# A fused two-layer transformer on one NeuronCore: a new hand-written order of 3,078 steps, other engines, PSUM banks and cross-engine turns, 76 waits of TensorE placed elsewhere, 17 waits added

## The chip, the cores and the metric

The kernel runs on one core of a Trainium2 chip. The metric is the device time of one execution in microseconds (us). The core has a matrix engine (PE in the profile, TensorE in words), whose weight loads are shown apart (PEld), a vector engine (DVE), an engine for activation functions (ACT), a general engine (POOL) and a queue that issues transfers (SP). Each engine runs its own list of instructions in order. They keep step by semaphores: an instruction can wait until a counter has reached a value.

## The reference, cut to what matters

```python
x = A_x                                           # [1, 2048, 512], bf16
for layer in range(2):                            # the same weights in both
    q, k, v = split(layernorm(x) @ wqkv)          # 32 heads of 16
    p = softmax(where(0 <= i - j < 256, q @ k.T / 4, -1e9))
    x = x + (p @ v) @ wo
    h = gelu(layernorm(x) @ w1 + b1)              # 512 -> 1792, tanh form
    x = x + h @ w2 + b2                           # 1792 -> 512
```

## The kernel before, in words

The 2,048 rows of x are 16 tiles of 128 rows. Both layers are laid end to end, so there are 32 tiles (tau 0 to 31). Attention works on pairs of tiles, 16 blocks b; its queries look back at most 256 positions, so a block needs the keys and values of itself and of the block before.

For a block: `layernorm` makes statistics (L618, L620), the reciprocal root on POOL (L630) and the normalised tile xn (L640), which is transposed by TensorE for the first four tiles and later by a DMA (L645). The products with wqkv go through `pe_group` (L666). `evac` brings Q and V from PSUM to SBUF, on DVE (L607) or, as its alternative, on ACT (L609). K is spread out by DVE with a parity mask (L700). V is copied a second time, shifted by 64 rows, by two DMAs per tile (Vs, L715).

The scores come in "visits". A visit fills four PSUM banks with 512 columns for each of four groups of 32 rows (L767, 8, 12 or 24 matmuls). Two exponentials on ACT, 128x1024 each, empty them into E (L774). There are 150 visits and 300 exponentials. DVE or POOL multiplies parts of E by a mask (L795). `pv` multiplies E with V and Vs (L819, 128 matmuls of 64x17 weights, or 64 in the first block of a layer, 32 times). DVE transposes the result (L828) and takes reciprocals (L832), DVE or POOL normalises it (L836), DVE transposes it back (L842); then follow the product with wo (L666) and the residual sum (L868).

The MLP runs in ten jobs of 2 or 4 tiles. `w1` makes 14 groups of 4 products (L666). Six of them get their bias on DVE (L891) and their gelu in pairs on ACT (L894), eight get both on ACT (L899). Then 14 products with w2 per tile (L666), with x + b2 made on POOL (L907) and the sum on DVE (L911). In the trace both w1 and w2 are called W_sb; the lists of instructions below call them W1_sb and W2_sb.

All products through L666 are called dense here: 128 rows by 128 weights. 1,058 of them have 512 columns and 736 have 256 (18 of the former are warm-up products on zeros, L559). Scores and PV use parts of the array, four or eight at once.

Nothing schedules this at run time. The code registers 3,078 steps in `_Plan.add`, each with its engine and the names it reads and writes. `_Plan.run` takes the order from the table `_ORDER`, the other engine for the steps in `_ALT`, and the PSUM bank of each allocation from `_BANKS`. `_TURNS` is a list of pairs (a, z): step a is made to write, and step z to read, a name of their own, so that z waits for a even where no data say so. `_Sched.op` then gives each step the waits that its names need and that its engine doesn't know to be over already; a wait passes on all that the awaited step knew. It emits them ahead of the step:

```python
for s, v in _sems:
    e.wait_ge(s, v)
ins = _fn(e)
ins.then_inc(_csem, _inc)
```

One wait rides on the step's first matmul; further ones become instructions of their own on TensorE's list, up to two waits in each. Before the change that list has 7,571 matmuls, each with a weight load, and 161 instructions that only wait.

## Time and profile before

| | |
|---|---|
| median of 3 runs | 439.43 us (439.15 to 439.68) |
| the profiled execution | 440.44 us, its span 438.9 us |
| PE busy | 412.5 us (94%) |
| ACT busy | 386.6 us (88%) |
| DVE busy | 335.6 us (76%) |
| POOL busy | 209.1 us (48%) |
| granted TensorE clock | 0.998 |

The span runs from the first to the last instruction of the program; 1.54 us of the profiled execution lie around it. PE's busy time holds matmuls that are pipelined, with modelled ends: a busy PE is not PE at its peak. What a product really takes is read from the starts of weight loads that follow each other.

### The profile page before, as it was taken

The page shows a single profiled execution, that of the slowest core. Times are in us where ns is not written, and L with a number is a line of the kernel's source. Part 1 is how long each engine was busy: PE and PEld are TensorE (multiplying, and loading weights), DVE is VectorE, ACT ScalarE, POOL GpSimd, SP SyncE. Part 2 cuts the span into 40 slices and gives each one's busy share as a digit, 9 for nine tenths or more (in the row PEclk, how much of TensorE's full clock was granted, in tenths as well). Part 3 has the DMA queues.
Part 4 walks back from the last instruction along what each step waited for, and adds up shares of the span by engine and source line. Part 5 has one row for each costly group of instructions (what it writes and reads, how often), then busy time and mean ns, then how long its engine had stood idle before and what let it go on. Part 6 is the DMA issues. An engine that isn't in the chain of part 4 may idle for free.

```text
span 438.9 us, 16863 instructions
## 1 busy us (share of the span) xinstructions
PE 412.5 (94%) x7497; PEld 227.9 (52%) x7571; DVE 335.6 (76%) x635; ACT 386.6 (88%) x458; POOL 209.1 (48%) x233
## 2 busy tenths in 40 slices
PE   8989999998699988999999999999999999999995
PEld 4555756554444544454454455454564554444662
DVE  6999878689867788976899687878877586655841
ACT  3999988999999899999999999999889989899442
POOL 4675263372555366731566344442443645635140
PEclk9999999999999999999999999999999999999999
DMA  7782812102300303212040111201322013003030
GB/s 234 216 210 39 221 32 52 38 21 40 58 3 13 52 4 46 32 34 44 10 94 2 25 27 28 52 1 33 43 55 50 1 31 82 7 0 76 3 108 25
DMA packets 49060, 23.51 MB, mean 54 GB/s; under 512 B 34268, under 2 KB 48988, under 8 KB 48988
## 3 DMA queue, kind: packets, MB, share of 16 engines
q1 hardware_dynamic: 48988, 22.43, 23.2%
q8 instruction: 60, 0.98, 1.0%
q14 instruction: 12, 0.10, 0.1%
HBM read 8.00 MB, written 2.10 MB: 23 GB/s over the span
## 4 chain that ended last, share of the span: by engine, by line
PE 76%; ACT 10%; DVE 6%; DMA 3%; issue 3%; POOL 1%; SPq 1%; POOLq 0%; DVEq 0%
PE ps L666 59%; ACT E L774 9%; PE ps L767 9%; PE ps L819 7%; DVE OD L828 1%; DVE KT L700 1%; POOL E L795 1%; DMA xnTA<-xn 1%; DMA xnTB<-xn 1%; DVE X L911 1%; DVE stat L618 1%; SPq L645 1%; ACT Va L609 0%; DMA X<-in_A_x_dram 0%; DVE E L795 0%
## 5 line engine op out<-in xcount | busy, mean ns | idle before, releaser
L774 ACT ACTIVATE E<-ps 128x1024 bf16<-128x1024 f32 x300 | 284.0, 1038 | 21.7 <-PE ps L767 20.2
L795 POOL TENSOR_TENSOR E<-E,mask 128x512 bf16<-128x512 bf16 (+2 forms) x112 | 121.6, 1097 | 107.7 <-ACT E L774 43.8
L666 PE MATMUL ps<-W_sb,gT 128*128 128x512 bf16 x415 | 106.5, 380 | 3.2 <-issue 2.5
L666 PE MATMUL ps<-xnTB,W_sb 128*128 128x512 bf16 (+1 forms) x542 | 105.5, 335 | 3.6 <-issue 1.6
L666 PEld LDWEIGHTS ps<-xnTB,W_sb 128*128 128x128 bf16 x560 | 52.0, 98 | 43.9 <-issue 4.3
L666 PE MATMUL ps<-xnTA,Wqkv_sb 128*128 128x256 bf16 x512 | 70.6, 273 | 2.2 <-DVE OD L828 1.1
L767 PE MATMUL ps<-QT,KT 32*128 32x128 bf16 (+3 forms) x1920 | 60.6, 231 | 4.9 <-ACT E L774 2.0
L795 DVE TENSOR_TENSOR E<-E,mask 128x512 bf16<-128x512 bf16 (+2 forms) x124 | 51.2, 438 | 14.1 <-ACT E L774 6.8
L666 PEld LDWEIGHTS ps<-W_sb,gT 128*128 128x128 bf16 x448 | 39.4, 98 | 43.1 <-issue 3.4
L828 DVE STREAM_TRANSPOSE OD<-ps 128x1024 f32<-128x1024 f32 x32 | 40.0, 1249 | 23.7 <-PE ps L819 23.5
L666 PEld LDWEIGHTS ps<-xnTA,Wqkv_sb 128*128 128x128 bf16 x512 | 46.3, 98 | 22.5 <-issue 3.2
L767 PEld LDWEIGHTS ps<-QT,KT 32*128 32x128 bf16 x1920 | 28.5, 92 | 51.3 <-ACT E L774 31.0
L899 ACT ACTIVATE gT<-ps,b1T 128x512 bf16<-128x512 f32 (+1 forms) x80 | 43.7, 606 | 10.1 <-PE ps L666 10.0
L907 POOL TENSOR_TENSOR Xb<-X,b2all 128x512 f32<-128x512 bf16 x32 | 36.8, 1152 | 20.4 <-DVE X L911 11.5
L618 DVE BATCH_NORM_STATS2 stat<-X 128x6 f32<-128x512 bf16 x64 | 43.3, 684 | 2.5 <-DMA X<-in_A_x_dram 1.7
L819 PE MATMUL ps<-E,Va 64*17 64x192 bf16 (+3 forms) x1920 | 39.9, 230 | 3.0 <-ACT E L774 1.3
L700 DVE TENSOR_TENSOR KT<-ps,parmask 128x1024 bf16<-128x1024 f32 x32 | 38.6, 1211 | 5.3 <-PE ps L666 5.1
L891 DVE TENSOR_SCALAR gT<-ps,b1T 128x512 bf16<-128x512 f32 (+1 forms) x60 | 36.8, 631 | 6.3 <-PE ps L666 5.9
L836 POOL TENSOR_TENSOR Nb<-OD,Rc 128x512 bf16<-128x512 f32 x18 | 19.0, 1056 | 42.9 <-DVE Rc L832 28.6
L819 PE MATMUL ps<-E,Vs 64*17 64x128 bf16 (+3 forms) x1920 | 39.2, 230 | 0.0
L630 POOL TENSOR_TENSOR rstd<-rstd,mhalf 128x2 f32<-128x2 f32 (+1 forms) x33 | 24.3, 736 | 28.9 <-DVE rstd L624 27.2
L911 DVE TENSOR_TENSOR X<-Xb,ps 128x512 bf16<-128x512 f32 x32 | 21.6, 682 | 19.2 <-PE ps L666 19.0
(49 smaller groups left out, 362.3 us busy)
## 6 DMA issues: line engine op xcount, KB each, us to landing
Vs<-Va SPq DMA_DIRECT2D x64, 68.0 KB, 2.9
W_sb<-in_B_w_dram SPq DMA_DIRECT2D x4, 512.0 KB, 4.6
out_dram<-X SPq DMA_DIRECT2D x16, 128.0 KB, 2.0
X<-in_A_x_dram SPq DMA_DIRECT2D x3, 512.0 KB, 6.6
Wqkv_sb<-in_A_wqkv_dram SPq DMA_DIRECT2D x4, 256.0 KB, 7.3
W_sb<-in_B_w_dram SPq DMA_DIRECT2D x1, 768.0 KB
W_sb<-in_B_w_dram SPq DMA_DIRECT2D x2, 384.0 KB, 5.2
Wqkv_sb<-in_A_wqkv_dram SPq DMA_DIRECT2D x1, 512.0 KB, 6.9
```

What stands on the lines that cost most here:

```text
L618: add("dve", lambda e, B, t=t, k6=k6: e.bn_stats(stat6[:, k6, :], X[:, t, :]), reads=["X%d" % t], writes=["st%d" % k6], key="bs%d" % (k + j))
L666: r = e.matmul(ps[:, B[g][0], cols], lhsT, rhs, start=st, stop=sp)
L700: add("dve", lambda e, B, g=g, i=i: e.tensor_tensor(out=KT[:, kb, 2 * i : 2 * i + 2].rearrange("p c m a q -> p a (c m) q"), in0=ps[:, B[g] ...
L767: x = e.matmul(ps[:, bk[r], o : o + n], KT[rows, kb, c, m].rearrange("p a q -> p (a q)"), QT[rows, c, q : q + n], start=True, stop=True)
L774: add("act", lambda e, B, g_=g_, gi=gi: e.activation(E[:, 2 * gi : 2 * gi + 2, e0 : e0 + 512], ps[:, B[g_][0] : B[g_][0] + 2, :], AF.Exp, ...
L795: fn = lambda e, B: e.tensor_tensor(out=Ew, in0=Ew, in1=Mw, op=ALU.mult)
L819: x = e.matmul(ps[32 * r : 32 * r + VW, B[g][par], c % 2 * 2 * P + lo : c % 2 * 2 * P + hi], V[rows, (2 * b + m // 2) % VR, c * HC + 2 * r ...
L828: add("dve", lambda e, B: e.transpose(OD[:, s].rearrange("p a c q -> p (a c q)"), ps[:, B[g][0] : B[g][0] + 2, :]), reads=["ps:" + g], wri ...
L891: add("dve", lambda e, B, g=g, fc=fc: e.tensor_scalar(out=gT[:, fc, c0 : c0 + M], in0=ps[:, B[g][0], 0:M], scalar1=b1T[:, fc : fc + 1], sc ...
L899: add("act", lambda e, B, g=g, fc=fc: e.activation(gT[:, fc, c0 : c0 + M], ps[:, B[g][0], 0:M], AF.Gelu_apprx_tanh, bias=b1T[:, fc : fc + ...
L907: add("pool", lambda e, B, t=t, xs=xs: e.tensor_tensor(out=Xb[:, xs, :], in0=X[:, t, :], in1=b2all[:], op=ALU.add), reads=["X%d" % t, "b2a ...
L911: add("dve", lambda e, B, g=g, t=t, xs=xs: e.tensor_tensor(out=X[:, t, :], in0=Xb[:, xs, :], in1=ps[:, B[g][0], :], op=ALU.add), reads=["X ...
```

## The change

The function that builds the steps stays as it is. The tables `_ORDER`, `_ALT`, `_TURNS` and `_BANKS` are replaced: 171 steps ran on their other engine and 165 do now, 82 of them the same ones. `_TURNS` had 182 pairs, all between DVE and POOL. It now has 168 of that kind and, at its end, 76 pairs whose second step is a dense product on TensorE; in 64 the first step is a DMA (47 copies of V and 17 transposes), in 12 it is an instruction of DVE, POOL or ACT. The first step stands 12 to 208 steps ahead of the second in the order. A new table `_PAD` names 17 dense products that get two waits on TensorE's own counter, for its first and second step, ahead of what else they wait for.

TensorE's list has 121 wait-only instructions instead of 161. It changes between dense products and scores or PV more often: 339 unbroken stretches of one kind (157 dense, 150 scores, 32 PV) instead of 332 (151, 149, 32). All matmuls are the same in number and shape. Of the evictions of V, ACT makes 8 (before 17) and DVE 24 (15); of Q, 9 (10) and 23 (22). Of the mask steps, POOL makes 116 (112) and DVE 120 (124); of the normalisations L836, POOL 21 (18) and DVE 11 (14).

```diff
 _ORDER = [
-    3, 14, 4, 0, 16, 33, 1, 18, 2, 34, 20, 37, 24, 32, 56, 36, 17, 35, 57, 25, 58, 60, 19, 61, 41, 59, 22, 62, 106,
...
 _ALT = [
-    62, 66, 69, 74, 94, 101, 108, 115, 120, 184, 191, 197, 201, 206, 210, 215, 219, 356, 363, 369, 373, 377, 378, 383,
...
+    69, 74, 108, 115, 120, 164, 184, 197, 201, 205, 210, 215, 219, 341, 356, 369, 373, 377, 378, 387, 388, 392, 397,
...
 _TURNS = [
...
+    2944, 2838, 2839, 2839, 2840, 2958, 2906, 2906, 2949, 2968, 2717, 2993, 2994, 2994, 2997, 2995, 3044, 103, 173,
+    149, 168, 416, 263, 264, 279, 528, 278, 192, 473, 185, 472, 193, 464, 646, 482, 648, 479, 704, 908, 357, 499, 365,
...
+_PAD = [
+    127, 761, 1289, 1123, 1124, 1116, 1197, 1673, 1403, 1404, 1405, 1406, 1231, 1250, 1251, 1433, 1556,
+]
+
 _BANKS = [
...
@@ -947,8 +957,19 @@
+        def held(fn):
+            def f(e):
+                e.wait_ge(S_.cnt_sem["pe"], 1)
+                e.wait_ge(S_.cnt_sem["pe"], 2)
+                return fn(e, B)
+            return f
+
+        pads = set(_PAD)
         for i in order:
             nd = PL.nodes[i]
+            if i in pads:
+                S_.op("pe", held(nd["fn"]), reads=phys(nd["reads"]), writes=phys(nd["writes"]))
+                continue
             S_.op(nd["eng"], lambda e, fn=nd["fn"]: fn(e, B), reads=phys(nd["reads"]), writes=phys(nd["writes"]), dma=nd["dma"])
```

Ten lines are added above the code, so a line number from L347 on is higher by 10 in the changed kernel (L666 becomes L676, L767 L777, L819 L829).

The first place is on PE, between the second PV of block 3 and the first PV of block 4. A row is a run of equal matmuls, with output, operands, shape and count; rows of 256, 192 + 128 and 128 + 64 columns with QT and KT are one visit each. Before, the twelve rows ahead of that PV:

```order
L666 MATMUL ps<-Wo_sb,OT 128x512 x4
L767 MATMUL ps<-QT,KT 128x192 x8
L767 MATMUL ps<-QT,KT 128x128 x4
L666 MATMUL ps<-Wo_sb,OT 128x512 x4
L767 MATMUL ps<-QT,KT 128x128 x8
L767 MATMUL ps<-QT,KT 128x64 x16
L666 MATMUL ps<-xnTA,Wqkv_sb 128x256 x8
L767 MATMUL ps<-QT,KT 128x256 x8
L666 MATMUL ps<-xnTA,Wqkv_sb 128x256 x8
L767 MATMUL ps<-QT,KT 128x256 x8
L767 MATMUL ps<-QT,KT 128x192 x8
L767 MATMUL ps<-QT,KT 128x128 x4
```

With the change, the eleven rows ahead of the same PV:

```order
L676 MATMUL ps<-Wo_sb,OT 128x512 x4
L676 MATMUL ps<-W2_sb,gT 128x512 x2
L777 MATMUL ps<-QT,KT 128x256 x8
L676 MATMUL ps<-W2_sb,gT 128x512 x6
L676 MATMUL ps<-Wo_sb,OT 128x512
L777 MATMUL ps<-QT,KT 128x256 x8
L676 MATMUL ps<-Wo_sb,OT 128x512 x3
L676 MATMUL ps<-xnTA,Wqkv_sb 128x256 x6
L777 MATMUL ps<-QT,KT 128x192 x8
L777 MATMUL ps<-QT,KT 128x128 x4
L676 MATMUL ps<-xnTA,Wqkv_sb 128x256 x4
```

Before, five visits stand with 8 dense products of 512 columns and 16 of 256, and two visits follow each other with nothing between. Now three visits stand with 16 of 512 and 10 of 256; products with w2, which came earlier before, lie between the scores.

The second place is on DVE at the very start: the first four tiles of x (the spdma counters tell of their landing) and the first two normalised tiles. Before:

```order
L618 BN_STATS stat6<-X 128x6 [waits cnt_spdma0]
L620 BN_AGGR statmv<-stat6 128x2 [waits cnt_dve]
L618 BN_STATS stat6<-X 128x6 [waits cnt_spdma1]
L620 BN_AGGR statmv<-stat6 128x2 [waits cnt_dve]
L624 TENSOR_SCALAR rstd<-statmv 128x1 [waits cnt_dve]
L618 BN_STATS stat6<-X 128x6 [waits cnt_spdma2]
L640 TENSOR_SCALAR xn<-X,statmv,rstd 128x512 [waits cnt_pool] x2
L618 BN_STATS stat6<-X 128x6
```

With the change:

```order
L628 BN_STATS stat6<-X 128x6 [waits cnt_spdma0]
L630 BN_AGGR statmv<-stat6 128x2 [waits cnt_dve]
L551 TENSOR_SCALAR pidx<-pidx 128x2 [waits cnt_pool]
L628 BN_STATS stat6<-X 128x6 [waits cnt_spdma1]
L630 BN_AGGR statmv<-stat6 128x2 [waits cnt_dve]
L628 BN_STATS stat6<-X 128x6 [waits cnt_spdma2]
L628 BN_STATS stat6<-X 128x6
L650 TENSOR_SCALAR xn<-X,statmv,rstd 128x512 [waits cnt_pool]
L650 TENSOR_SCALAR xn<-X,statmv,rstd 128x512
```

The statistics of the fourth tile moved ahead of the first two normalised tiles.

The third place is on PE, ahead of a PV step, with the counters that each row waits for. Before, ahead of the first PV of block 3:

```order
L666 MATMUL ps<-W2_sb,gT 128x512 x2
L666 MATMUL ps<-Wqkv_sb,xnTA 128x512 [waits cnt_dve]
L666 MATMUL ps<-Wqkv_sb,xnTA 128x512 x3
L767 MATMUL ps<-QT,KT 128x192 [waits cnt_act]
L767 MATMUL ps<-QT,KT 128x192 x7
L767 MATMUL ps<-QT,KT 128x128 x4
L666 MATMUL ps<-W2_sb,gT 128x512 x4
L819 MATMUL ps<-E,Va 17x64 [waits cnt_spdma5,cnt_dve,cnt_spdma2,cnt_act,cnt_pool,cnt_spdma7]
```

With the change, ahead of the same PV:

```order
L676 MATMUL ps<-W2_sb,gT 128x512 [waits cnt_spdma7]
L676 MATMUL ps<-W2_sb,gT 128x512 [waits cnt_spdma5]
L676 MATMUL ps<-xnTA,Wqkv_sb 128x256 [waits cnt_pool]
L676 MATMUL ps<-xnTA,Wqkv_sb 128x256
L777 MATMUL ps<-QT,KT 128x128 [waits cnt_act]
L777 MATMUL ps<-QT,KT 128x128 x7
L777 MATMUL ps<-QT,KT 128x64 x16
L676 MATMUL ps<-xnTA,Wqkv_sb 128x256 x2
L829 MATMUL ps<-E,Va 17x64 [waits cnt_act,cnt_dve]
```

Six waits at the PV became two; the others ride singly on dense products ahead of it.

397 rows, old and new, of tables (_ALT, _BANKS, _ORDER, _TURNS) are left out of this document.

## The prediction

> **What bounds the kernel now.** I began with the page: busy times and the chain of waits.
>
> ```profile
> span 438.9 us, 16863 instructions
> PE 412.5 (94%) x7497; PEld 227.9 (52%) x7571; DVE 335.6 (76%) x635; ACT 386.6 (88%) x458; POOL 209.1 (48%) x233
> ...
> PE 76%; ACT 10%; DVE 6%; DMA 3%; issue 3%; POOL 1%; SPq 1%; POOLq 0%; DVEq 0%
> ```
>
> TensorE leads, ACT is close behind. Since a busy PE is not PE at its peak, I took the true price of its work from the starts of weight loads in the timeline, at places where nothing is late.
>
> ```profile
> 152.63 0.12 PEld L767 LDWEIGHTS ps<-QT,KT 32*128 32x128 bf16 x8 [0.42 <-ACT E L774]
> 152.96 0.98 PEld L666 LDWEIGHTS ps<-W_sb,gT 128*128 128x128 bf16 x6 [0.21 <-issue]
> 154.36 0.12 PEld L767 LDWEIGHTS ps<-QT,KT 32*128 32x128 bf16 x8 [0.42 <-ACT E L774]
> ...
> 291.82 0.11 PEld L819 LDWEIGHTS ps<-E,Va 64*17 64x17 bf16 x8 [0.32 <-DVE E L795]
> ...
> 293.06 0.20 PEld L767 LDWEIGHTS ps<-QT,KT 32*128 32x128 bf16 x12
> 293.39 1.41 PEld L666 LDWEIGHTS ps<-W_sb,gT 128*128 128x128 bf16 x8
> 294.92 0.97 PEld L666 LDWEIGHTS ps<-xnTA,Wqkv_sb 128*128 128x128 bf16 x8
> 296.10 0.29 PEld L767 LDWEIGHTS ps<-QT,KT 32*128 32x128 bf16 x24 [0.21 <-ACT E L774]
> ```
>
> Six products of 512 columns take 1.40 us up to the next visit, and eight of 512 with eight of 256 take 2.71: both fit 0.216 for 512, 0.108 for 256, and 0.105 for leaving a dense stretch. A visit takes 0.33: 0.216 for 512 columns in each of four row groups, and 0.114 for leaving it. A PV of 128 matmuls takes 1.24. Over the whole list: 1,058 x 0.216 + 736 x 0.108 + 0.9 (transposes) + 150 x 0.216 + 28 x 1.24 + 4 x 0.7 (the short PVs) + 151 x 0.105 + 149 x 0.114 = 411.4 us. The last product ends at 434.4, so TensorE stands still for some 23 us, and 4.5 us follow it (a sum, a store). The windows below are cut where visits 0 (10.96), 20, 45, 65 (172.06) and 145 begin.
>
> ```profile
> core 0: us, PE busy (x) PEld busy (x) DVE busy (x) ACT busy (x) POOL busy (x), PEclk, DMA share, GB/s
> 0.00:10.96 10.96, 8.94 (x58) 4.95 (x58) 7.17 (x20) 3.56 (x5) 4.64 (x15) 1.00 0.79 234
> 10.96:63.62 52.66, 48.98 (x894) 31.26 (x904) 46.81 (x86) 49.47 (x62) 31.95 (x41) 1.00 0.61 149
> 63.62:121.46 57.84, 51.33 (x1173) 30.49 (x1181) 47.87 (x93) 55.48 (x68) 26.27 (x31) 1.00 0.21 40
> 121.46:172.06 50.60, 47.05 (x939) 24.62 (x948) 38.65 (x74) 47.51 (x54) 28.17 (x28) 1.00 0.14 21
> 172.06:396.08 224.02, 218.37 (x3912) 113.50 (x3954) 173.79 (x322) 209.20 (x239) 106.12 (x110) 1.00 0.17 34
> ```
>
> Up to visit 65 ACT sets the pace: it is busy 49.47 + 55.48 + 47.51 = 152.5 of 161.1 us, while TensorE's list holds only 145.5 us of work there and idles 15.6. From visit 65 on TensorE sets it: 258.9 us of work in 262.3, with 3.4 idle. Three questions follow: what ACT has to do before visit 65, how much it stands idle there, and how much TensorE work is left after.
>
> ```profile
> ACT E L774 <- PE ps L767: 7.1, 14, 1.0
> ACT QT L609 <- PE ps L666: 0.8, 1, 0.8
> ACT Va L609 <- PE ps L666: 0.4, 1, 0.4
> ACT gT L899 <- PE ps L666: 0.4, 1, 0.4
> ```
>
> These are ACT's waits from 10.96 to 172.06 (total, times, longest): 8.7 us, nearly all for scores.
>
> **Term 1, ACT's work before visit 65: -2.4 us.** By the order, ACT evicts V there 3 times instead of 9 and Q 5 times instead of 3; exponentials and gelus are the same.
>
> ```profile
> L774 ACT ACTIVATE E<-ps 128x1024 bf16<-128x1024 f32 x130 | 122.7, 1044 | 7.5 <-PE ps L767 7.1
> ...
> L609 ACT ACTIVATE Va<-ps 128x512 bf16<-128x512 f32 x9 | 5.5, 609 | 0.5 <-PE ps L666 0.4
> ...
> L609 ACT ACTIVATE QT<-ps 128x512 bf16<-128x512 f32 x4 | 2.3, 610 | 0.8 <-PE ps L666 0.8
> ```
>
> That is -6 x 0.609 + 2 x 0.610 = -2.4, on the engine that sets the pace. The evictions go to DVE, which has room (busy 133.3 of 161.1) but is in the path of Q, K and V; that is the slower rival below. If DVE's room were gone the 2.4 would come back. The other moves between DVE and POOL (masks, normalisations) land on POOL, 48% busy.
>
> **Term 2, the start: +0.6 us.** DVE's order puts the statistics of the fourth tile ahead of the first two normalised tiles.
>
> ```profile
> 4.67 0.68 DVE L618 BATCH_NORM_STATS2 stat<-X 128x6 f32<-128x512 bf16 x1
> 5.27 0.72 DVE L640 TENSOR_SCALAR xn<-X,statmv,rstd 128x512 bf16<-128x512 bf16 x2
> ```
>
> One more 0.68 ahead of 5.27; the transposes, 26 projections and K's eviction follow in a row to visit 0. Bounds: 0 (a landing decides) and 0.9 (with the small DVE operation also moved there). I take 0.6, near the row.
>
> **Term 3, TensorE's work after visit 65: +2.15 us.** The list now leaves dense work for later: between visits 0 and 65 stand 463 products (in units of 512 columns) instead of 475, -2.6 us; ahead of visit 0, 0.65 more (18 warm-ups instead of 15); and 5 more stretches before visit 65, +0.55. So 1.4 us less is done by visit 65. In all there are 7 more stretches, +0.77. What is left is 1.4 + 0.75 = 2.15 more, where TensorE has no cover.
>
> **Term 4, ACT's idle time before visit 65: -2.5 us.** Visits come in time when each has dense work to overlap, and not too much. At the place shown first, five visits stood with 8 x 0.216 + 16 x 0.108 = 3.5 us of dense work, against 10 exponentials of 122.7 / 130 = 0.944, 9.4 us; now three visits with 4.5 against 5.7. Each step that TensorE must wait out also has more in front of it. In TensorE's own work, from the last score of a PV to that PV: second of block 3 2.6 to 4.0 us, first of block 4 3.1 to 6.3, second of block 6 3.0 to 5.3. From the last wo product to the first w1 product: third MLP job 5.0 to 7.6, fourth 7.8 to 9.3. Two of these waits in the trace:
>
> ```profile
> 160.53 0.11 PEld L666 LDWEIGHTS ps<-xnTA,Wqkv_sb 128*128 128x128 bf16 x2 [1.29 <-DVE OD L828]
> ...
> 173.57 0.11 PEld L666 LDWEIGHTS ps<-xnTB,W_sb 128*128 128x128 bf16 x2 [0.85 <-DMA xnTB<-xn]
> ```
>
> While TensorE stands there, it makes no scores and ACT runs dry. What ACT will idle can't be counted, only bounded: -6.5 (two of the 8.7 stay) to +2.4 (it idles away what it was spared). I take less than half of the lower end, -2.5, because other chains are shorter than before (block 0 second PV to its wo product 4.5 to 3.7, block 4 9.1 to 4.9).
>
> **Term 5, TensorE's late idle time: -0.8 us.** Of the 3.4 us, one piece has no wait in the program at all:
>
> ```profile
> 106.04 0.09 PEld L767 LDWEIGHTS ps<-QT,KT 32*128 32x128 bf16 x2 [0.21 <-DVE Rc L832]
> 106.79 0.20 PEld L767 LDWEIGHTS ps<-QT,KT 32*128 32x128 bf16 x10 [0.65 <-issue]
> ...
> 379.17 1.62 PEld L666 LDWEIGHTS ps<-xnTB,W_sb 128*128 128x128 bf16 x9
> 381.48 0.98 PEld L666 LDWEIGHTS ps<-xnTB,W_sb 128*128 128x128 bf16 x6 [0.68 <-issue]
> ...
> q8 instruction: 60, 0.98, 1.0%
> ```
>
> Both halts split a step of equal products. 60 packets of instructions for a list of 15,303 is one for 255, and the halts stand at its instructions 3,776 and 14,016, 40 x 256 apart. So a block of 256 instructions arrives late when the one before it ran out in 2.9 or 3.1 us of work (6.8 on average). With the change the shortest blocks hold 2.6, 3.2 and 3.2 us, no longer than before, but all before visit 65, where ACT sets the pace; after it the shortest holds 3.6. So the 0.6 at 381.48 goes, and I take 0.2 more of the rest. Bounds: 0 and -2.6.
>
> The Trainium skill, "Runtime: NRT & Kernel Launch", section "Instruction fetch mechanics", says that blocks of 256 instructions are fetched ahead and that the cost of crossing a block is mostly hidden. By that rule the positions of the blocks would be worth nothing here and the sum 0.6 higher, 437.1. The trace agrees on the block and, at 381.48, not on the hiding.
>
> **At nothing: the moved waits and the 17 added.** A PV with six waits starts 0.97 us after four dense products began, which is 4 x 0.216 + 0.105, just like one with two waits (three products, 0.75):
>
> ```profile
> 95.04 0.55 PEld L666 LDWEIGHTS ps<-W_sb,gT 128*128 128x128 bf16 x4
> 96.01 0.09 PEld L819 LDWEIGHTS ps<-E,Va 64*17 64x17 bf16 x3 [0.42 <-issue]
> ...
> 209.77 0.33 PEld L666 LDWEIGHTS ps<-W_sb,gT 128*128 128x128 bf16 x3 [0.21 <-issue]
> 210.52 0.11 PEld L819 LDWEIGHTS ps<-E,Va 64*17 64x17 bf16 x8 [0.42 <-issue]
> ```
>
> The sequencer takes waits while the dense products ahead still run, so taking them from PVs gains nothing either. A moved wait costs only if what it awaits is not over; then the products behind it, and the visit behind those, are late. The nearest stands 12 steps after what it awaits, some 1.7 us at 439 us for 3,078 steps, and most stand 40 and more. The 17 added wait for TensorE's first two steps. Without cover each could cost a weight load's 0.1 us, 1.7 in all, less 4 for the 40 that the list loses on balance; I take 0. New banks and the 168 pairs between DVE and POOL have no row of their own; what they cost is in the bounds of term 4.
>
> **The sum.** Span: visit 0 at 10.96 + 0.6; then 152.5 - 2.4 + 8.7 - 2.5 = 156.3 (161.2 by these terms before); then 261.05 + 2.6 (before 258.9 + 3.4); then 4.5. In all -2.4 + 0.6 + 2.15 - 2.5 - 0.8 = -2.95. The span of 438.9 becomes 436.0. The profiled execution took 440.44, and the median of the runs is 439.43, so I take the difference to the median: **436.5 us**.
>
> **Rivals.** First, the idle times stay as they are and only the counted terms act: -2.4 + 0.6 + 2.15 = +0.35, 439.8. For it: chains of waits tend to close up elsewhere when one is relaxed; against it: nearly every long wait I looked at between visits 35 and 65 gets more cover. Second, much more is won: ACT idles 2.7 instead of 8.7 and TensorE 1.4 late instead of 3.4: 0.35 - 6 - 2 = -7.65, 431.8. For it: ACT's longest single wait is only 1.0 us, so small shifts close many; against it: the new order was not freed of short chains. Third, slower: the V evictions now on DVE stand in its queue ahead of Q and K, whose arrival the scores await, and ACT idles 2.4 more, as much as it was spared:
>
> ```profile
> 104.01:115.70 11.69, 8.50 (x134) 4.45 (x120) 10.95 (x21) 11.38 (x15) 5.01 (x6) 1.00 0.36 55
> ```
>
> In this stretch DVE is busy 10.95 of 11.69, hardly less than ACT. Then 0.6 + 2.15 = +2.75, 442.2; it decides once ACT idles over 11 us before visit 65. Against it: DVE's work per stretch, counted by the order, changes by less than 2 us anywhere before visit 65. Last, the instruction blocks: if only their positions counted for anything, the change would be worth its 0.6 against 0.77 of new switches, no change.
>
> **How the numbers follow.** The forecast has 0.50 (434 to 438.5), the large gain 0.20, no change 0.16 (the first rival and the blocks), slower 0.14. A measurement of this kernel tells about 0.2% (0.9 us) from no change. So faster 0.70, within 0.2% 0.16, slower 0.14. The range reaches to the large gain's middle and halfway between the first rival and the slower one: 432.0 to 441.0.
>
> **What would show it.** On the changed kernel: visit 0 near 11.5; visit 65 near 168; ACT's waits between them near 6 us; products with w2 between the visits ahead of block 4's first PV with no ACT wait over 0.5; no halt by "issue" over 0.3 us after visit 65; 2 us more TensorE work after it. It is wrong if visit 65 comes at 172 or later, or if ACT idles 9 us and more before it, or if waits on DMAs appear at dense products.

## The result, and the profile after

The changed kernel takes 433.55 us (433.44 to 434.34, 4 runs) against 439.36 (439.15 to 439.68, 4 runs): a ratio of 0.9868, 95% interval 0.9849 to 0.9887. It is 5.8 us faster, twice the 2.9 that was forecast, and inside the range. Run once more, it was 0.9862 (0.9840 to 0.9884).

The profiled execution took 433.44 us, its span is 431.7. Busy times and the chain of waits on the page of the changed kernel:

```profile
span 431.7 us, 16809 instructions
...
PE 410.6 (95%) x7500; PEld 228.0 (53%) x7571; DVE 336.0 (78%) x637; ACT 379.6 (88%) x447; POOL 217.3 (50%) x242
...
PE 68%; ACT 19%; DVE 7%; issue 2%; DMA 1%; POOL 1%; SPq 1%; DVEq 0%
```

ACT's share of the chain has doubled, from 10 to 19%, and the chain's "issue" is down from 3 to 2%. The windows of the changed kernel, cut at visit 0 (12.34) and visit 65 (165.53):

```profile
core 0: us, PE busy (x) PEld busy (x) DVE busy (x) ACT busy (x) POOL busy (x), PEclk, DMA share, GB/s
0.00:12.34 12.34, 10.58 (x60) 5.78 (x61) 7.83 (x22) 3.07 (x4) 6.08 (x20) 1.00 0.83 241
12.34:165.53 153.19, 143.53 (x2996) 84.74 (x3019) 131.65 (x249) 149.00 (x177) 90.28 (x96) 1.00 0.31 71
165.53:431.70 266.17, 256.45 (x4459) 137.45 (x4492) 196.49 (x368) 227.52 (x267) 120.96 (x126) 1.00 0.17 36
```

Between the two visits ACT is busy for 149.0 of 153.2 us; before it was 152.5 of 161.1. Its groups there (busy us, mean ns of one, and idle time ahead with its releaser):

```profile
L784 ACT ACTIVATE E<-ps 128x1024 bf16<-128x1024 f32 x130 | 121.4, 1060 | 4.4 <-PE ps L777 4.4
...
L619 ACT ACTIVATE QT<-ps 128x512 bf16<-128x512 f32 x5 | 3.1, 621 | 0.0
L619 ACT ACTIVATE Va<-ps 128x512 bf16<-128x512 f32 x3 | 1.9, 619 | 0.0
```

So the evictions are the 3 and 5 that the order promised, and the waits for scores are 4.4 us instead of 7.1.

What that looks like, from ACT's timeline between 53 and 70 us (visits 16 to 22), the kernel before and then the changed one:

```profile
53.93 1.02 ACT L774 ACTIVATE E<-ps 128x1024 bf16<-128x1024 f32 x1
55.39 0.60 ACT L609 ACTIVATE Va<-ps 128x512 bf16<-128x512 f32 x1 [0.44 <-PE ps L666]
55.88 1.02 ACT L774 ACTIVATE E<-ps 128x1024 bf16<-128x1024 f32 x1
57.68 5.72 ACT L774 ACTIVATE E<-ps 128x1024 bf16<-128x1024 f32 x6 [0.78 <-PE ps L767]
63.29 1.09 ACT L609 ACTIVATE QT<-ps 128x512 bf16<-128x512 f32 x2
64.24 1.98 ACT L774 ACTIVATE E<-ps 128x1024 bf16<-128x1024 f32 x2
66.89 1.94 ACT L774 ACTIVATE E<-ps 128x1024 bf16<-128x1024 f32 x2 [0.67 <-PE ps L767]
69.52 1.02 ACT L774 ACTIVATE E<-ps 128x1024 bf16<-128x1024 f32 x1 [0.69 <-PE ps L767]
```

```profile
53.84 14.79 ACT L784 ACTIVATE E<-ps 128x1024 bf16<-128x1024 f32 x16
```

Before, four gaps and three evictions lie between 13 exponentials; now 16 exponentials follow each other. Between visits 0 and 65 of the kernel before, nine of ACT's waits for scores are of 0.5 us or more. Ahead of eight of them TensorE had 2.4 to 4.1 us of work since the visit before, by the prices of the prediction, and stood still for 0.4 at most: ACT waited for scores that TensorE had not come to, not for a TensorE that was itself kept waiting.

Where the 7.2 us of the two spans went, by the starts of visits in the two timelines. Some 1 us of them is that the profiled execution of before lies 1.0 above its median.

| | before | after | change | forecast |
|---|---|---|---|---|
| visit 0 | 10.96 | 12.34 | +1.4 | +0.6 |
| visit 0 to visit 65 | 161.1 | 153.2 | -7.9 | -4.9 |
| visit 65 to the last weight load | 261.8 | 262.7 | +0.9 | +1.35 |
| from there to the end | 5.1 | 3.5 | -1.6 | 0 |

Two things were not in the sum as they are: the stage up to visit 65 won 3 us more, and the end itself 1.6. How much of the latter other executions share is taken up in the section on the tail. A second profile of the changed kernel has visit 0 at 12.33, visit 65 at 166.35 and the last weight load at 428.76; its stage between the two visits is 154.0 us, so 7.1 are won there instead of 7.9.

### The profile page after: what moved, and what is told of

Read it like the earlier page. It is cut to its first block, busy times and chain, and to the rows that moved or that the text cites. A ratio compares the mean times of both kernels' runs of the same rounds, so it can differ in the third digit from the quotient of the medians.

```text
span 431.7 us, 16809 instructions
## 1 busy us (share of the span) xinstructions
PE 410.6 (95%) x7500; PEld 228.0 (53%) x7571; DVE 336.0 (78%) x637; ACT 379.6 (88%) x447; POOL 217.3 (50%) x242
## 4 chain that ended last, share of the span: by engine, by line
PE 68%; ACT 19%; DVE 7%; issue 2%; DMA 1%; POOL 1%; SPq 1%; DVEq 0%
PE ps L676 53%; ACT E L784 15%; PE ps L777 7%; PE ps L829 6%; PE ps L569 2%; ACT gT L909 1%; DMA Vs<-Va 1%; DVE OD L838 1%; ACT gT L904 1%; DVE E L805 1%; DVE QT L617 1%; POOL Nb L846 1%; ACT L909 1%; DVE stat L628 1%; DVE KT L710 1%
## 5 line engine op out<-in xcount | busy, mean ns | idle before, releaser
L805 POOL TENSOR_TENSOR E<-E,mask 128x512 bf16<-128x512 bf16 (+2 forms) x116 | 128.3, 1120 | 105.2 <-DVE E L805 50.4
L676 PE MATMUL ps<-W_sb,gT 128*128 128x512 bf16 x413 | 105.6, 380 | 4.6 <-issue 3.7
L676 PE MATMUL ps<-xnTB,W_sb 128*128 128x512 bf16 (+1 forms) x547 | 101.7, 336 | 1.7 <-issue 0.8
L676 PEld LDWEIGHTS ps<-xnTB,W_sb 128*128 128x128 bf16 x560 | 52.4, 98 | 42.9 <-issue 1.6
L676 PE MATMUL ps<-xnTA,Wqkv_sb 128*128 128x256 bf16 x512 | 67.5, 273 | 1.3 <-DVE xnTA L617 0.5
L777 PE MATMUL ps<-QT,KT 32*128 32x128 bf16 (+3 forms) x1920 | 60.1, 231 | 3.1 <-ACT E L784 1.4
L676 PEld LDWEIGHTS ps<-W_sb,gT 128*128 128x128 bf16 x448 | 38.3, 98 | 43.7 <-issue 4.0
L805 DVE TENSOR_TENSOR E<-E,mask 128x512 bf16<-128x512 bf16 (+2 forms) x120 | 49.2, 434 | 15.0 <-POOL E L805 6.6
L676 PEld LDWEIGHTS ps<-xnTA,Wqkv_sb 128*128 128x128 bf16 x512 | 47.4, 98 | 17.9 <-issue 2.5
L777 PEld LDWEIGHTS ps<-QT,KT 32*128 32x128 bf16 x1920 | 28.2, 92 | 50.5 <-ACT E L784 31.9
L829 PE MATMUL ps<-E,Va 64*17 64x192 bf16 (+3 forms) x1920 | 39.5, 230 | 2.2 <-ACT E L784 1.0
L829 PE MATMUL ps<-E,Vs 64*17 64x128 bf16 (+3 forms) x1920 | 38.8, 230 | 0.0
L846 POOL TENSOR_TENSOR Nb<-OD,Rc 128x512 bf16<-128x512 f32 x21 | 22.2, 1056 | 32.5 <-DVE Rc L842 16.0
L650 DVE TENSOR_SCALAR xn<-X,statmv,rstd 128x512 bf16<-128x512 bf16 x64 | 24.4, 402 | 13.4 <-POOL rstd L640 8.3
```

Of the source, the lines that this page charges most:

```text
L676: r = e.matmul(ps[:, B[g][0], cols], lhsT, rhs, start=st, stop=sp)
L777: x = e.matmul(ps[:, bk[r], o : o + n], KT[rows, kb, c, m].rearrange("p a q -> p (a q)"), QT[rows, c, q : q + n], start=True, stop=True)
L805: fn = lambda e, B: e.tensor_tensor(out=Ew, in0=Ew, in1=Mw, op=ALU.mult)
L829: x = e.matmul(ps[32 * r : 32 * r + VW, B[g][par], c % 2 * 2 * P + lo : c % 2 * 2 * P + hi], V[rows, (2 * b + m // 2) % VR, c * HC + 2 * r ...
L846: return e.tensor_tensor(out=Nb[:, s, :].rearrange("p (k a d) -> p a k d", a=2, d=Dh), in0=sums[:, :, :, 0:Dh], in1=rc[:, :, :, None].to_b ...
```

## The experiments

Each ratio is to runs of the kernel before, made beside it. Stage times are from one profiled execution each; visit 20 varies by about 0.6 us either way between executions of the same order, so smaller differences are not read.

### The tail: one packet of instructions in the way of the last store

```diff
 _TURNS = [
...
+    2889, 2995, 2906, 1309, 1260, 1308, 1259, 1316, 1258, 1315, 1433, 1429, 1727, 1428, 1726, 1436, 1668, 1435, 1667,
+    1686, 1637, 1685, 1636, 1693, 1616, 1692, 1615, 1781, 1916, 1780, 1915, 1788, 1931, 1787, 1930, 2042, 1986, 2041,
...
```

From 1309 on these are new pairs: a copy of V, and the dense product that now waits for it.

> The kernel before, with 31 pairs added to its turns: waits of late PVs for landed copies of V now stand at dense products ahead of them, so TensorE's list has 15,288 instructions instead of 15,304 and no longer passes 15,296 = 192 + 59 x 256. Theory (the 60th packet): in the trace of before the 60th packet of instructions takes one of the 16 DMA engines from 435.44 to 436.82 us, and the last store's part on that engine ends at 437.9, the others at 436.6. Without that packet the last store lands some 1.1 us sooner: 438.3 us, 59 packets, and some 3.9 us from the last weight load to the end instead of 5.1. Rival (two stores): before issues its last two stores 0.65 us apart, and they share the DMA engines; then the time stays at 439.4. Moved waits as such: both theories give them nothing.

Measured: ratio 0.9971 (0.9955 to 0.9988), 1.3 us less; the tail is 3.55 us instead of 5.09. The DMA view of the last microseconds, first of the kernel before, then of this one (packets by queue; KB each and median us from issue to landing):

```profile
q1 hardware_dynamic: 288, 0.26, 15.8%
q8 instruction: 1, 0.02, 1.7%
issues: line engine op xcount, KB each, median us to landing
out_dram<-X SPq DMA_DIRECT2D x2, 128.0 KB, 3.0
```

```profile
q1 hardware_dynamic: 288, 0.26, 22.7%
issues: line engine op xcount, KB each, median us to landing
out_dram<-X SPq DMA_DIRECT2D x2, 128.0 KB, 1.7
```

The stores are the same two, 0.65 us apart in both; without the packet they land after 1.7 us instead of 3.0. But the tail is not all that this edit changed. The moved waits shift earlier block boundaries too: the block ahead of instruction 14,016 now holds some 4.7 us of work instead of 3.1, and the halt at 381.48 that the prediction shows is gone. The products that it split run through:

```profile
379.41 4.65 PEld L669 LDWEIGHTS ps<-xnTB,W_sb 128*128 128x128 bf16 x23
```

So the 1.3 us are the tail and that halt together. Now the other way round, on the changed kernel, by pads at the last products:

```diff
 _PAD = [
-    127, 761, 1289, 1123, 1124, 1116, 1197, 1673, 1403, 1404, 1405, 1406, 1231, 1250, 1251, 1433, 1556,
+    127, 761, 1289, 1123, 1124, 1116, 1197, 1673, 1403, 1404, 1405, 1406, 1231, 1250, 1251, 1433, 1556, 3062, 3063,
+    3064, 3065, 3066, 3067, 3068, 3069, 3070, 3071, 3072, 3073, 3074, 3075, 3045, 3046, 3047, 3048, 3049, 3050, 3051,
+    3052, 3053, 3054, 3055, 3056, 3057, 3058,
 ]
```

These are 28; the kernels with 40, 48 and 60 name more products near the end.

> The changed kernel, with 28 more waits of TensorE on its own first steps, at the last 28 dense products: 15,292 instructions, still 59 packets, and no instruction ahead of 15,040 moves. Theory: redundant waits cost nothing where the sequencer is ahead: 433.6 us (up to 0.3 more). Rival: each costs a weight load's 0.1 us: 436.4.

> The same with 40 such waits: 15,304 instructions as in the kernel before, so the list passes 15,296 some 8 instructions ahead of its end. Theory (the 60th packet): a 60th packet comes just as the last store runs, and the end is 1.1 us later than with 28: 434.7 us, with one of the 16 DMA engines ending about 1.3 us after the others. Rival (two stores, or nothing): as with 28, 433.6; if each wait costs 0.1: 437.6.

> The same with 60 such waits: 15,324 instructions, so 15,296 is passed 28 instructions and some 2 us ahead of the end. Theory (the 60th packet, in the way of the last store): the packet is over before the last store starts, and the end is as with 28: 433.6 us, up to 0.3 more. Rival (a 60th packet costs, wherever it comes): 434.7. If each wait costs 0.1 us: 439.6.

> The changed kernel with 48 more waits on TensorE's own steps at its end: 15,312 instructions, so that 15,296 is passed 16 instructions ahead of the end, between the runs with 60 (28 ahead, its packet over before the last store) and 40 (8 ahead, its packet after the last store). Theory (a packet of instructions costs only where it meets the last store): if the 60th packet comes between 429.5 and 431.5, one of the 16 DMA engines ends 1 us or more after the others and the tail from the last weight load grows from 3.5 to 4.5 or more; if it comes at another time the tail is 3.5. Rival: 3.5 in any case.

Measured: 0.9873, 0.9863, 0.9858 and 0.9888 (0.9853 to 0.9923, two runs only) of the kernel before, against 0.9868 and 0.9862 without these pads. The tail is 3.5 us in all four. With 40, 48 and 60 pads there is a 60th packet, but it came at 433.46 (after the last store, which ended at 431.7), 428.54 and 426.55 (ahead of it). So no dose made the packet meet the last store, and with 40 pads the forecast of 1.1 us more than with 28 failed for that reason. With 48 pads the packet ran beside the store before the last, which landed 2.9 us after its issue; in the changed kernel the same store takes 1.7:

```profile
out_dram<-X SPq DMA_DIRECT2D x1, 128.0 KB, 2.9
```

The last store was issued 3 us after that one and still took 1.7. So in these runs a 60th packet that missed the last store left the tail as it was, and 60 redundant waits cost nothing that an interval of 0.2% either way would show. Three later profiles of a list of the same length in the old order (the section on V) had their 60th packet at 443.68, 444.40 and 441.66, after the last store; their tails were 3.56 and 3.57. That settles against the two stores: same list length, same stores, and 5.1 only where the packet came between.

It also bounds what the tail is worth. In those three profiles, and with 40 pads, the packet started 5.0 to 6.0 us after TensorE came to the last boundary; in the profile of the kernel before it started after 2.3. How often it meets the store in other executions of that kernel is not known, and this one lies 1.0 us above the median. The halt at instruction 14,016 took 0.6 to 1.0 us in four profiles of the old order. Of the 1.3 us that the first edit saved, that leaves 0.3 to 0.7 for the tail, an estimate from these numbers.

### The moved waits: what they do is place the blocks

The last 76 pairs of the turns taken out; then the 17 pads too; then the pads alone:

```diff
-_PAD = [
-    127, 761, 1289, 1123, 1124, 1116, 1197, 1673, 1403, 1404, 1405, 1406, 1231, 1250, 1251, 1433, 1556,
-]
+_PAD = []
 _TURNS = [
...
-    2944, 2838, 2839, 2839, 2840, 2958, 2906, 2906, 2949, 2968, 2717, 2993, 2994, 2994, 2997, 2995, 3044, 103, 173,
...
+    2944, 2838, 2839, 2839, 2840, 2958, 2906, 2906, 2949, 2968, 2717, 2993, 2994, 2994, 2997, 2995, 3044,
```

> The changed kernel without the 76 new pairs: its waits stand at PVs and scores again, the 17 added waits stay, and the list has 15,304 instructions. Theory (instruction blocks): with the boundaries then at other places, eight blocks of 256 after visit 65 hold 1.66, 1.95, 2.48, 2.72, 2.84, 2.86, 2.92 and 3.01 us of TensorE's own work. In the trace of before a block arrived late when the one ahead of it held 3.14 or less, by 0.57 us at 3.14, so about 3.6 us are needed: the eight halts add 1.94 + 1.65 + 1.12 + 0.88 + 0.76 + 0.74 + 0.68 + 0.59 = 8.4 us: 442 us, with halts by "issue" at each. Rival (the waits themselves, as the prediction has it: they cost nothing at either place): 433.6. Rival (waits at PVs cost, some 0.05 us each): 437.

> The same, and without the 17 added waits: 15,287 instructions, the waits at PVs and scores as in the run without the pairs. Theory (instruction blocks): the short blocks after visit 65 hold 2.84, 3.26, 3.31 and 3.56 us: 0.76 + 0.34 + 0.29 + 0.04 = 1.4 us: 435.0. Rival (the waits cost nothing): 433.6. Rival (waits at PVs cost): as without the pairs, 437.

> The changed kernel without the 17 added waits alone: 15,247 instructions. Theory (instruction blocks): one block after visit 65 becomes short, 2.45 us at instruction 14,016, and halts TensorE for 1.15 us near 390: 434.7 us. Rival (added waits are worth nothing): 433.6.

Measured: without the pairs 444.02 us, ratio 1.0095 (1.0077 to 1.0112), slower than the kernel before and 10 us above the changed one. The theory of this run had 442, from its eight halts alone. Without pairs and pads 0.9940 (0.9928 to 0.9952), 3.2 above. Without the pads 0.9871 (0.9851 to 0.9892), the same as with them.

Two of the halts in the run without the pairs (weight loads on TensorE; the bracket is the idle time ahead):

```profile
335.62 0.11 PEld L668 LDWEIGHTS ps<-xnTB,W_sb 128*128 128x128 bf16 x2
338.12 1.41 PEld L668 LDWEIGHTS ps<-xnTB,W_sb 128*128 128x128 bf16 x8 [2.39 <-issue]
...
400.44 0.11 PEld L668 LDWEIGHTS ps<-W_sb,gT 128*128 128x128 bf16 x2 [0.21 <-DVE stat L620]
402.50 1.82 PEld L668 LDWEIGHTS ps<-W_sb,gT 128*128 128x128 bf16 x9 [1.95 <-issue]
```

Each splits a row of equal products at an instruction 256 n + 192, as in the trace of before, but they are up to 2.4 us long. From visit 65 to the last weight load this run needs 271.0 us, the changed kernel 262.7: 8.3 more, where the sum over the short blocks was 8.4. (That it agrees to 0.1 us is in part luck: the trace has nine halts of 0.5 us and more at block boundaries there, some 9.6 us by the prices, one of them behind a block of 3.2 us that the theory had left out, and other waits were shorter for it.) Without pairs and pads it is 263.8: 1.1 more, forecast 1.4. In both runs the waits stand at PVs and scores again. So the sums leave little for the waits as such; what they change is the positions.

The rest of the 10 and the 3.2 us was lost before visit 65 (167.4 and 168.0 instead of 165.5), which the expectations had not counted. Blocks are short there too (some 2.6 and 2.9 us ahead of instructions 3,776 and 4,288), and in the second run TensorE also waited 1.4 us for a transposed tile, of which more below.

The run without pads was forecast wrong: its block of 2.45 us at 14,016 gave no halt. In its trace the packet for that block starts at 376.54, although TensorE runs instruction 13,760, the boundary before, only at 379.7. Ahead of that boundary stand 26 dense products in a row, and the packet is 3 us ahead of TensorE. So here a short block behind a dense stretch didn't hurt, and the working by TensorE's own work alone was too strict.

### V on DVE or on ACT

Six evictions of V (nodes 94, 101, 191, 363, 560, 937) taken out of the list of steps on ACT in the kernel before, and put into it in the changed one:

```diff
 _ALT = [
-    62, 66, 69, 74, 94, 101, 108, 115, 120, 184, 191, 197, 201, 206, 210, 215, 219, 356, 363, 369, 373, 377, 378, 383,
...
+    62, 66, 69, 74, 108, 115, 120, 184, 197, 201, 206, 210, 215, 219, 356, 369, 373, 377, 378, 383, 392, 397, 401, 411,
...
```

> The kernel before, with six evictions of V ahead of visit 65 (tiles 0, 1, 5, 7, 9 and 13) on DVE instead of ACT, order and list of TensorE as they were. Theory (ACT sets the pace up to visit 65): 6 x 0.609 = 3.65 us less for ACT, visit 65 at 168.4 instead of 172.1, and since TensorE sets the pace from there with nothing to spare, the end as much sooner: 435.8 us. Rival (DVE's queue is in the path of Q, K and V): ACT idles as much more as it is spared, 439.4 us or above, with ACT's waits between the visits at 12 us instead of 8.7.

> The changed kernel with the same six evictions of V (tiles 0, 1, 5, 7, 9 and 13) put back on ACT, order and TensorE's list as they are: the other side of the run that took them off ACT in the kernel before. Theory (ACT sets the pace up to visit 65): 6 x 0.61 = 3.65 us more for ACT, of which its 4.2 us of waits take up one at most: visit 65 at 168.2 to 169.2 instead of 165.5, the end 2.7 to 3.65 later, 436.3 to 437.2 us. Rival (what counts is how well the chains behind DVE are covered, and who evicts V is worth nothing, as the run in the kernel before suggests): 433.6, ACT's waits 3 us or more shorter.

Measured: in the kernel before 1.0080 (1.0062 to 1.0098), 3.4 us slower, visit 65 at 175.8 instead of 172.1. In the changed kernel 0.9916 (0.9897 to 0.9935), some 2.2 us slower, visit 65 at 168.3. That is the visit 65 of its theory, but 1.5 us of it are a wait of another kind (the section on the copies of V). So the same edit loses in one order, and its reverse loses in the other. To find where the old order loses it, four evictions (tiles 0 and 1 back on ACT), and the six once more:

> The kernel before with four evictions of V on DVE instead of ACT (tiles 5, 7, 9 and 13); tiles 0 and 1 stay on ACT. With six, visit 20 came 2.2 to 3.1 us later, not sooner, and in its trace DVE evicts V of tiles 1 and 0 at 14.81 and 17.76, ahead of a spread of K and of the Q for which TensorE then waits 1.07 us at 19.69. Theory (DVE's queue at the start): without these two, visit 20 comes at 64.5 or sooner instead of 66.7, and the time is at most that of the kernel before. Rival (the loss is made further on, at tiles 7 and 9, between 50 and 60 us, where a packet of instructions came late and the visit at 56.17 with it): visit 20 at 66 or later and the time 2 us or more above the kernel before.

> The kernel before with all six evictions on DVE once more. Theory (DVE's queue): visit 20 at 66 or later again, some 3 us above the kernel before beside it, whether or not a packet of instructions comes late at 56 us. Rival (that packet was chance): without it visit 20 comes 1.3 us sooner than at 66.7. Also: the list has 15,304 instructions, and the tail from the last weight load is 3.5 us where the 60th packet misses the last store and 5 where it meets it.

Measured: 1.0044 (1.0025 to 1.0063) and 1.0066 (1.0045 to 1.0087). With four the time is still 1.9 us above the kernel before, where the theory had it no higher: most of the loss is not made at the start, and the rival holds. Since six cost 1.0 us more than four, in intervals that overlap, the start may have a share. In the profile with four, visit 20 came at 68.1, but that can't be set against the others: the execution took 445.03 us, 3.4 above the median of its kernel, and TensorE's clock fell in it ahead of visit 20 (last section). With six once more, visit 20 came at 65.7, just under the 66 of the theory, and the packet came late again, so this run does not part theory and rival. TensorE's weight loads between 53 and 56 us, with six once more, then with four:

```profile
53.63 0.10 PEld L666 LDWEIGHTS ps<-Wo_sb,OT 128*128 128x128 bf16 x1
55.14 0.15 PEld L767 LDWEIGHTS ps<-QT,KT 32*128 32x128 bf16 x8 [1.41 <-issue]
```

```profile
53.54 0.10 PEld L666 LDWEIGHTS ps<-Wo_sb,OT 128*128 128x128 bf16 x1
55.87 0.15 PEld L767 LDWEIGHTS ps<-QT,KT 32*128 32x128 bf16 x8 [2.23 <-DVE statmv L620]
```

This visit stands at instruction 1,728, a block boundary. In the traces the packet for it started 2.95, 2.42 (six) and 3.08 us (four) after TensorE crossed the boundary before; in the two profiles of the old order with V on ACT 1.37 and 1.65, in the fifteen of the changed order 0.8 to 1.6. (The row of the second names a step of DVE that ended just then; the list has no such wait.) In the late cases TensorE crossed at 50.0 to 50.8, 0.9 to 1.0 us after two loads of weights had begun to be issued; in the two others at 48.55, ahead of them at 49.22, and at 49.45, 0.3 after. In the changed order no load of weights is issued between 47 and 52.5. So late packets beside these loads are shown three times. That the loads delay them is argued from this order of times and was not tried; nor is it settled what makes TensorE cross later. A second gap follows at once: ACT has run dry, and 16 dense products stand ahead of the next visit.

### Evenness of TensorE's work between visits

```diff
 _ORDER = [
...
-    955, 738, 958, 938, 739, 740, 637, 960, 741, 635, 742, 638, 510, 956, 743, 511, 959, 968, 749, 512, 1023, 513,
...
+    512, 513, 514, 515, 516, 517, 955, 738, 958, 938, 739, 740, 637, 960, 741, 635, 742, 638, 956, 743, 959, 968, 749,
...
```

510 to 517 are the eight products; they stood after 638, the last of them just ahead of 744.

> The changed kernel with eight products with w2 of tile 3 put two visits sooner: between the visits 38 and 39 stand then 14 products of 512 columns instead of 6, later ones lose them, and no instruction block after visit 45 moves. Theory (ACT's idle time comes from uneven TensorE work between the visits): 14 x 0.216 + 0.44 = 3.5 us of work against two exponentials of 0.944 and what ACT still has in hand, another 0.9 at most: ACT stands idle 0.7 to 1.6 us more there, never makes it up, and the end is as much later, 434.3 to 435.2 us. Rival (idle time comes from waits for DVE and transfers alone): 433.6.

Measured: 0.9935 (0.9914 to 0.9956), 2.9 us above the changed kernel and more than the 0.7 to 1.6 of the theory. ACT at that place, from 103 us on, in the changed kernel and with the lump:

```profile
102.15 7.44 ACT L784 ACTIVATE E<-ps 128x1024 bf16<-128x1024 f32 x8
```

```profile
107.35 2.85 ACT L784 ACTIVATE E<-ps 128x1024 bf16<-128x1024 f32 x3 [1.48 <-PE ps L777]
```

In the changed kernel the exponentials follow each other without a gap; with the lump there is one of 1.48. Visits 35 to 45 take 21.27 us instead of 19.69, 1.6 more, as the theory has it; the eight products are 1.73 us of work. From visit 45 on the stages are the same length as in the changed kernel (48.84 and 48.84 to visit 65, 262.76 and 262.68 to the last weight load): nothing is made up. The other 0.9 us that the profile is later stood at visit 35 already, ahead of the edit, and the profile lies 0.8 under the median of its kernel; what makes up the rest of the 2.9 us was not traced.

### The start

DVE's and TensorE's first steps in another order, and one turn (61, 67) taken out:

```diff
 _ORDER = [
-    3, 14, 4, 34, 13, 21, 20, 33, 19, 27, 37, 17, 25, 0, 36, 18, 29, 1, 16, 41, 58, 24, 2, 32, 35, 15, 23, 59, 5, 56,
...
+    3, 14, 4, 34, 13, 33, 19, 27, 37, 17, 25, 0, 36, 1, 16, 41, 58, 24, 2, 32, 35, 15, 23, 59, 5, 56, 31, 62, 46, 63,
+    57, 67, 104, 38, 60, 61, 40, 64, 106, 39, 68, 21, 29, 20, 49, 107, 105, 65, 28, 18, 26, 22, 30, 108, 69, 45, 109,
...
```

> The changed kernel with another start: 10 instead of 18 warm-up products ahead of the first transpose, the others around it; the first two normalised tiles ahead of the third and fourth tile's statistics on DVE; the first spread of K ahead of the copy of tile 2's transpose. Theory (a late start costs its full length, since ACT sets the pace from visit 0 on): visit 0 some 1.5 us sooner, 10.8 instead of 12.3, and the end as much, 432.0 us. Rival (between visits 0 and 20 something else is late anyway, a transfer or DVE): visit 0 sooner, visit 20 and the end as now, 433.6.

Measured: 0.9883 (0.9858 to 0.9909), no gain. Visit 0 came at 12.29: the first spread of K was sooner, but the copy of tile 2's transpose behind it held up products that stand ahead of visit 0. As an edit it failed, and says nothing of the theory. For that the changed kernel was run once more, unedited:

> The changed kernel as it is, once more, beside the three runs that follow. Theory (a start or a landing that varies between executions is not handed on): whatever visit 0 is this time (11.1 to 12.3 in the runs so far), visit 20 comes at 60.3 to 61.1, visit 65 near 165.5 when the third MLP job's first product finds its input landed, and 1.6 us later when it doesn't. Rival (a start that is late costs its full length): visit 20 and the end move with visit 0, us for us.

Measured: 0.9862, visit 0 at 12.33, visit 20 at 61.41, visit 65 at 166.35, the last two 0.3 and 0.8 later than the theory had them though there was no wait for a transfer at visit 45. Seven profiles share one order up to visit 20. Their visits 0 and 20 were 12.34 and 60.62, 12.33 and 61.41, 12.15 and 60.58, 12.10 and 60.22, 12.05 and 61.05, 11.60 and 60.10, 11.47 and 61.10: a visit 0 that is 0.9 sooner brings nothing at visit 20. What does set visit 20 was not tried.

### The copies of V

Loads 54 and 55 behind 142, the last of the three copies:

```diff
 _ORDER = [
...
-    208, 374, 376, 215, 44, 175, 176, 177, 209, 55, 178, 375, 379, 210, 179, 149, 380, 220, 373, 54, 211, 148, 381,
...
+    208, 374, 376, 215, 44, 175, 176, 177, 209, 178, 375, 379, 210, 179, 149, 380, 220, 373, 211, 148, 381, 384, 221,
+    377, 141, 386, 160, 142, 54, 55, 161, 162, 222, 163, 383, 385, 223, 394, 359, 382, 360, 164, 361, 224, 362, 388,
...
```

> The changed kernel with the loads of b2 and of the last four tiles of x put behind three copies of V (tiles 2 and 3) on SP's queue. In the trace of the changed kernel the second PV waits 1.0 us for such a copy at 36.06, 5.8 us after its issue, while the loads run. Theory (ACT runs dry behind that wait): the wait goes, and with it ACT's gaps of 0.59 at 38.49 and 0.81 at 41.51; visit 20 comes 1.0 us sooner and so does the end, 432.6 us. Rival (the gaps are the PV's own 1.24 us in front of a visit): 433.6.

Measured: 0.9875 (0.9851 to 0.9899), no gain. The wait for the copy went, and of ACT's two gaps the first; the second stayed, with 0.75. Visit 20 came 0.35 sooner, less than it varies, and at visit 45 TensorE waited (its waits there: total, times, longest):

```profile
PEld ps L676 <- DMA xnTB<-xn: 1.8, 1, 1.8
```

This wait for the transposed input of the third MLP job, 1.1 to 1.8 us, stood in seven profiles of the changed order with small edits, and in neither profile of the changed kernel itself nor in three more that have the same steps there (without the pads, with 60 more, with another start). So it varies between executions. In the run with V back on ACT it was 1.5 of the 2.8 us at visit 65. The six evictions, all ahead of visit 45, had cost that run only 0.7 to 1.5 us there (118.2 against 117.5 and 116.7), well under their 3.65. By the medians it is 2.2 us, some of it that wait.

### The input of the third MLP job sooner

Tile 7's products with wo (744 to 747) ahead of the rest of tile 3's with w2 (512 to 517), and the steps behind them sooner; in a second kernel the loads moved as above too:

```diff
 _ORDER = [
...
-    970, 514, 952, 515, 961, 516, 517, 744, 969, 636, 518, 972, 745, 957, 746, 974, 962, 747, 911, 748, 912, 951, 913,
...
+    958, 938, 739, 740, 637, 960, 741, 635, 742, 638, 510, 956, 743, 511, 959, 968, 744, 745, 746, 747, 749, 512, 1023,
+    513, 970, 514, 952, 515, 961, 748, 751, 750, 752, 753, 754, 516, 517, 969, 636, 518, 972, 957, 974, 962, 757, 758,
...
```

> The changed kernel with tile 7's four products with wo ahead of the last six products with w2 of tile 3, and the residual sum, statistics and normalised tiles 38 and 39 behind them sooner on DVE, so that the transposed input of the third MLP job is issued some 1.5 us sooner. In three of five runs of the changed order TensorE waited 1.4 to 1.8 us for it at visit 45. Theory (that wait is what varies): no wait for a transfer there in this run, visit 65 no later than 165.6, the median 0.5 to 1.0 us under that of the changed kernel beside it. Rival (the masks that DVE now makes later hold up the PV behind visit 42): a wait there for DVE, no gain or a loss of up to 1 us.

> Both moves together: the one for the third MLP job, and the loads of b2 and of the last tiles of x behind the copies of V. Theory: another 0.35 us by visit 20, as in the run that had the loads moved alone: 0.8 to 1.3 us under the changed kernel beside it. Rival: as with the first move alone.

Measured: 0.9892 (0.9868 to 0.9917) and 0.9891 (0.9870 to 0.9912), 1.3 us above the changed kernel beside them. The wait for the transfer is gone in both. Another has taken its place, for the sum that frees a PSUM bank, which the edit had put later to make room:

```profile
PEld ps L676 <- DVE X L921: 1.1, 1, 1.1
```

The rival had foreseen a loss, by the masks; it was the sum. No kernel that was run beats the changed one by more than its interval.

## Why the prediction was right or wrong

The sign, the range and the stages were right: ACT up to visit 65, TensorE after it. The size was off by a factor of two. The step that failed is in term 4, "I take less than half of the lower end": 2.5 us of ACT's idle time were to go, and 4.4 went, because most of ACT's waits in the old order stood behind stretches of 2.4 to 4.1 us of TensorE's own work, which the new order has evened out. "Then 4.5", the end put down as fixed, failed too, by a smaller and less certain amount. Of the signs named at the end, ACT's waits (4.4 instead of "near 6") and visit 65 (165.5 instead of "near 168") went further than forecast; the 2 us more TensorE work and the missing halts after visit 65 came as named. Term by term:

- **Term 1**, ACT's work: -2.4 by the evictions, measured -2.8 (their two groups, 7.8 us before and 5.0 after). The count was misread: the row quoted there has four evictions of Q, not three, and with five in the new order the sum is -6 x 0.609 + 0.610 = -3.0. For all that ACT does between the visits it is -3.5. The groups overlap, so their differences don't simply add up, but the exponentials have a part in it that the term left out: together they take 121.4 us instead of 122.7, since one alone takes 1.02 us and 16 without a gap took 14.79, 0.92 each. Pricing a moved eviction at its full length is not borne out by the runs of that move alone: in the old order it costs 2.9 to 3.4 us, and in the new one taking it back costs 2.2 of 3.65, part of it a wait that varies. The third rival (V on DVE gives a slower kernel) is what happens without the new order; the mechanism that it named, DVE's queue, has at most a part in it.
- **Term 2**, the start: +0.6 was forecast, +1.4 came, and it should have been 0: in the new order visit 20 doesn't follow visit 0.
- **Term 3**, TensorE's work after visit 65: +2.15. By the same prices the two lists give 2.16. Right. (The prices of the whole list add up to 411.7, not 411.4; nothing else hangs on it.)
- **Term 4**, ACT's idle time: this is the term that was mis-sized. -2.5 was forecast inside -6.5 to +2.4; 8.6 became 4.2, so -4.4, and 4.6 in the second profile, so -4.0. The mechanism it names, cover between visits, is what the lump shows: 1.73 us of work at the wrong place costs 1.6, and in that run nothing gave it back. But the place that I showed for it, ahead of block 4's first PV, was one where ACT was busy for 11.38 of 11.69 us by the row quoted there: little could be won in it. And the longer cover for waits of TensorE was not the main thing, since eight of ACT's nine longer waits stood behind a TensorE that worked. Evenness was: of the 65 stretches from one visit to the next, three hold the w1 products of a job, and of the others 13 hold more than 2.5 us of TensorE's work in the old order and 3 in the new, by the prices; the two exponentials of a visit take 1.9. The clearest is between visits 16 and 17: the old order has there 16 products of 512 columns and two of 256, 16 x 0.216 + 2 x 0.108 = 3.7 us, the new one four and eight, 1.7.
- **Term 5**, TensorE's late idle time: -0.8, measured from visit 65 to the last weight load as 262.7 less 261.0 of work against 261.8 less 258.9, so 1.7 instead of 2.9: -1.2. The halt at 381.48 is gone, as forecast.
- **"Then 4.5"**: the tail was taken as fixed. It shrank by 1.6 us between the two profiles; how much of that the medians hold is open, 0.3 to 0.7 by the estimate above. The row that told it was quoted in the prediction: 60 packets for a list of 15,303, the last of them for a handful of instructions.
- **The moved waits at nothing**: right for the waits, wrong for the part. Without the pairs the new order would be slower than the old one, by its blocks (1.0095); without pairs and pads it keeps a little under half of the gain (0.9940). The rival "only the blocks count" compared positions before and after, both of them good, and not with the positions that the new order has by itself.

The 5.8 us add up so: visit 65 stands 5.7 to 6.5 us sooner in the two profiles of the changed kernel (forecast 4.3), the stage behind it is 0.7 to 0.9 longer although a halt of 0.6 is gone (forecast 1.35), and that leaves 0.2 to 0.8 for the tail. What stands ahead of visit 65 is ACT's work and idle time together, and no run here could part them further.

## What to carry to other kernels

Price work that you move off the pacing engine by what that engine then does, not by the work: in these runs six evictions of 3.65 us together were a loss of 3 us in one order and worth 2.2 at most in the other. Spread the other engine's work so that no stretch between two inputs is longer than what the pacing engine has in hand. Where a list runs through in order, count its instructions: find the blocks of 256 that run out fastest and the boundary nearest the end, and shift them with redundant waits, which cost nothing measurable here.

## What the runs showed of the hardware that was not expected

- A packet of instructions shares the DMA engines with data. The store that one met landed 1.2 to 1.3 us later than without (3.0 and 2.9 instead of 1.7); where it came 2 us ahead of the last store or 2 us after it, the tail stayed at 3.5.
- TensorE's instruction blocks: where a block held less work, TensorE still took 3.3 to 4.1 us from one boundary to the next, and halted for the difference, up to 2.4 us in one piece. In the run without the pairs, the stage with eight short blocks grew by 8.3 us, against 8.4 worked out. The Trainium skill, "Runtime: NRT & Kernel Launch", section "Instruction fetch mechanics", calls the crossing mostly hidden. In these traces it is hidden only where the block ahead holds enough work, or where the packet was fetched early, behind a dense stretch.
- Redundant waits cost nothing that could be measured: 60 of them at the last dense products gave 0.9858, none 0.9862 and 0.9868.
- TensorE's clock fell in the middle of a run. With four evictions on DVE, after the 2.23 us idle shown above, its products took 0.43 us each from 57.0 to 60.3 instead of 0.216, as the first warm-up products do. Windows of that run (the number behind the POOL column is the granted clock):

```profile
54.00:56.00 2.00, 0.10 (x4) 0.13 (x8) 0.84 (x3) 1.31 (x2) 0.95 (x3) 1.00 0.09 21
56.00:58.00 2.00, 2.00 (x15) 0.84 (x12) 1.23 (x1) 1.65 (x2) 0.69 (x1) 0.69 0.04 8
58.00:60.00 2.00, 2.00 (x6) 0.62 (x5) 0.60 (x1) 0.29 (x1) 0.00 (x0) 0.50 0.00 0
60.00:62.00 2.00, 2.00 (x20) 0.84 (x18) 1.97 (x5) 0.00 (x0) 1.18 (x2) 0.96 0.15 31
```

  Eight products at 0.43 instead of 0.216 are 1.7 us. The two slowest of this kernel's 12 runs, 445.03 and 444.75 us, are the two with a mean granted clock of 0.996; the others have 1.0 and 440.0 to 442.2. An idle time of 2.39 us in the run without the pairs left the clock at 1.00. So a stall of 2.2 us can cost nearly as much again behind it, and need not.
